# An S5 filter gated with linear attention on one core: the gate's logit as a column of K's weight, the skip term as products for all tiles, named buffers, and another list of the order

## The chip, the cores and the metric

The kernel runs on one core of a Trainium2 chip. The metric is the device time of one execution in microseconds. In the profile PE is the matrix engine (TensorE), PEld its loading of the stationary operand, DVE the vector engine, ACT the scalar engine, POOL the engine GpSimd and SP the engine that here only issues DMAs.

## The reference

```python
x = A_x                                            # [1, 2048, 512]
g = sigmoid((x * gate_w).sum(-1, keepdims=True))   # one number for each row
# a: S5 filter, 512 complex states
Lam_bar = exp(exp(log_dt) * Lam)                   # Lam = Lambda_re + 1j * Lambda_im
B_bar = ((Lam_bar - 1) / Lam)[:, None] * (B_re + 1j * B_im)
h[t] = Lam_bar * h[t - 1] + B_bar @ x[t]           # over the 2048 rows
a = 2 * real(h @ (C_re + 1j * C_im).T) + x * Dskip
# b: linear attention, 32 heads of 16
q, k, v = split(x @ wqkv)
pq, pk = q @ w_phi, k @ w_phi                      # per head, 16 x 16
phi = concat(softmax(p), softmax(-p))              # 32 features, for q and k
b = (phi_q @ (phi_k.T @ v)) / (phi_q @ sum(phi_k) + 1e-6) @ wo
out = g * a + (1 - g) * b
```

All inputs and the output are bf16.

## The kernel before, in words

The 2048 rows are taken as 16 tiles of 128. Row t belongs to residue t mod 8, and a tile holds the rows of one residue, half of them each. `xT` holds x transposed, with the 512 columns of x on the partitions in four pieces, and is the stationary operand of most products.

**The attention.** K and Q aren't built from `wqkv` and `w_phi` one after the other. The two weights are folded into one at the start (tokens `f0` to `f3` for K, `w0` to `w3` for Q, line 441ff.), and since a softmax doesn't change when one number is taken from all logits of a head, only 15 differences of each head are computed: 32 x 15 = 480 columns, in 8 blocks of 60. The product for a tile (`k0` to `k15`, `q0` to `q15`, line 493) is evacuated from PSUM into `Xq`, whose row has 8 blocks of 64: four zeros, then the 60 differences. K is handled in five groups of tiles (`KGROUPS`), Q in four (`G0` to `G3`). For a group, DVE takes the maximum and minimum over the features of a head as a tree (tokens `x` and `n`, line 544) and subtracts (lines 555, 561), ACT exponentiates (`e`, line 567), and DVE and POOL's adding DMAs sum (`s`). K's features times V with a column of ones, `vx`, are accumulated over all tiles into two banks of PSUM (`a0` to `a4`, line 627). Q's features are transposed by DMAs from the queue of SP into `phT` (line 613). Q's rows in `Xq` take the place of K's.

**The gate.** Beside the KV product, each tile has four products of one column (line 631): a piece of `xT` against a column `gw_b` of the gate's weight, into spare columns of the second PSUM bank. `st_G` (line 802) clamps the negated logit into `nge` and makes the gate `G` of it, for all tiles at once. The attention's reciprocal carries exp(-logit) as a bias (line 901), so that a product with the gate at the very end does for both halves.

**The filter.** Rows of eight residues turn the recurrence into one over 256 steps. `b` and `g` are its input products, `p`, `h`, `H`, `c`, `l` and `z` scale, rotate and scan the states; products with a diagonal are scaled copies on ACT or DVE (`scaled`, lines 444 and 446), and sums of large tiles are adding DMAs that POOL issues (line 529).

**The output.** For a tile, `y` accumulates eight products of 512 columns (states against C, line 875) in one bank, `o` computes the attention's numerators and denominators into two other banks (line 894), ACT takes the logarithm `ld` and the exponential `rd` (lines 898, 901), DVE multiplies into `on` (line 907), SP's queue transposes `on` of two tiles into `oT` (token `O`, line 930), and `t` adds four products with Wo to y's bank and evacuates it times `G` into `ot` (lines 943 to 951), which `R` stores. The skip term x * Dskip comes in two ways. For twelve tiles `y` adds four products of `xT` with a diagonal matrix `Dd` (line 882). For the four tiles of `XD`, 8 to 11, x is loaded once more, DVE computes `xd` = x * G * Dskip (line 913), and the evacuation adds it (line 947).

**What sets the order.** Each token of the list `ORDER` runs one more piece of a generator. `@` gives the PSUM banks, and `:D` puts the piece's evacuation or scaled copy on DVE, otherwise on ACT. The instructions go to their engines in the order of the list, and each engine keeps it:

```python
for tok in ORDER.split():
    tok, _, banks = tok.partition("@")
    tok, _, eng = tok.partition(":")
    sel["eng"] = "dve" if eng == "D" else "act"
    sel["banks"] = [int(b) for b in banks]
    next(st[tok])
```

At the start, `Z` are warm-up products on zeros, `W` and `T` transposes on PE of K's weight and of two tiles of x, `V` and `V2` transposes of small vectors (`vec_n`: the filter's three; `vec_m`: Dskip and the gate's weight). `Lx`, `Lb`, `Lc` and so on are loads; the transposing ones are issued by SP.

Of the kernel before, what the change touches and what calls it, by code (L numbers as in the profile page):

```python
# [24 lines left out]
B:D Lk Lk Z@0 Lx Z Z Z Z Z Z W00@1 Z B B B W01@2 W01 W01:D W00 W00 W10@0 Lx W11@3 Lx T0@4 B W11 T0 f1@2 Lx Lx f0@1 f0  # L25
W10:D f1:D T1@5 T1:D f2@3 f2 f3@0 f3:D k0@6 x0z:D Lx k1@7 V@3 V P U U k1 k1 k0 k0 P k3@3 P2 P P2 U P2 U k6@2 P2 P2 x0
Lx Lb Lx Lb P4 n0 P4 k3 x0 V2@6 P4 V2 P3 i3 gw P2 n0 P3 k5@7 x0 i3 x0 Lc k5 k9@3 k9 i0 Ld k2@0 M n0 i3 i3 k10@1 i3
k4@3 i0 M k2 i0 i0 i0 M Lb k10 i2 M k6 n0 k4 k7@0 k7 i2 Lb k8@7 i1 i2 x0 i1 i1 k13@6 M2 k11@0 n0 i2 k8 i1 x1 n1 x1 D
n1 x1 b200@1 i2 i1 L i0:D x1 D c1:D n1 Lc Lc i3:D n1 k11 e0 b010@7 b010 c0:D x1 n1 i2:D b200 x2 s0 c0:D s0 k12@3 k12
x2 g200@2 g200 n2 c1 b100@0 s0 b100 x2 b001@5 n2 Lv b000@7 Lc i1 b000 b111@4 b111 x2 n2 s0 n2 g000@2 b001 s0 c3:D  # L30
b011@3 b101@7 e1 x2 n2 g000 g000 Lx g001@5 g001 x3 s1 v1@4 b011 c3 s0 c2:D c2:D c1:D k14@2 g010@3 g010 Lo e2 x3 n3 s1
k13 D v0@0 v1 s1 g011@1 x3 c3:D g011 x3 g001 g011 v0 e2 k15@0 g011 g010 c0:D Lq Lq g010 s1 n3 k14 w2@6 c3 s0 D k15 n3
a0@54 s2 a0 g011 x3 n3 g011 Ld g010 g201@2 b101 Ld n3 s1 w2 g010 z0 b201@1 b201 z0 b110@7 n4 s1 x4 g101@3 g201 l2:D s2
s2 x4 n4 e3 z0 z0 w1@6 w1 b110 g100@2 g100 g101 g101 g100 s2 s2 s2 g111@1 l2:D l2:D g111 n4 g110@0 g110 e3 g110 g111
v2@2 v3@3 x4 n4 g110 g111 g111 g110 l2:D z0 v2 z0 v3 w3@2 s1 z0 g111 s3 g110 w0@7 w3 a1 a1 x4 c1 g301@6 z0 z1 z1 x4 w0
c2 g301 s3 g300@2 g300 z0 q3@7 q3 n4 e4 v5@6 z0 s2 s2 q2@2 s3 e4 q0@7 q0 z1 z1 l2:D z1 H0:D z1 s3 z1 z1 s4 v4@3 v4 q2
# [42 lines left out]
def kernel(  # L79
# [779 lines left out]
    def st_y(n):  # L859
# [23 lines left out]
        if n not in XD:  # L883
            yield
# [138 lines left out]
```

## Time and profile before

| | before |
|---|---|
| time of the runs, median (lowest to highest), 3 runs | 148.97 us (148.59 to 149.18) |
| the profiled execution: its span | 147.2 us |
| PE busy | 140.8 us, 96% |
| DVE busy | 135.1 us, 92% |
| ACT busy | 123.4 us, 84% |
| POOL busy | 45.4 us, 31% |
| packets of the transposing and plain DMAs of SP and ACT (queue q1) | 15.05 MB, 52.7% of 16 engines |
| granted clock of PE | 1.00 in all slices |

The span is the profiled execution's own time from its first to its last instruction; the profile gives no other time for that execution, and the runs' median stands 1.8 us above it. A row of the profile names a line of the kernel, an engine, an operation and tiles with their shapes. An engine is busy while an instruction runs; waits are idle times with the instruction that ended them. [...]

### The profile page before, as it was taken

How to read it: one execution, taken by the hardware profiler on the slowest of the kernel's cores; microseconds unless marked ns; L12 is line 12 of the kernel's file. 1: busy time of each engine (PE TensorE's matmuls, PEld its weight loads, DVE VectorE, ACT ScalarE, POOL GpSimd, SP SyncE). 2: the span in 40 equal slices, each digit the busy share in tenths (PEclk: the TensorE clock that was granted, in tenths of full speed). 3: DMA queues.
4: the chain of work that ended last, by engine and by line, in shares of the span. 5: the costliest groups of instructions: out<-in, count | busy, mean ns of one | idle time of the engine just before them, and what ended most of it. 6: DMA issues, size and time to landing. Idle time of an engine off the chain costs nothing.

```text
span 147.2 us, 2881 instructions
## 1 busy us (share of the span) xinstructions
PE 140.8 (96%) x1014; PEld 73.3 (50%) x1014; DVE 135.1 (92%) x330; ACT 123.4 (84%) x222; POOL 45.4 (31%) x61
## 2 busy tenths in 40 slices
PE   6999999999999999999999999999979999999990
PEld 2744444444544644554454656545445554545650
DVE  2879999999999999999999999999998999979740
ACT  3479999999999999999999999999988997912110
POOL 7503600003138195797545353051003003000000
PEclk9999999999999999999999999999999999999999
DMA  5999998990846586789878969969988999999643
GB/s 123 233 184 170 181 179 160 239 290 2 195 94 90 88 114 99 80 127 169 131 111 141 144 90 191 123 126 164 208 179 153 192 214 159 199 180 271 129 111 114
DMA packets 56047, 22.63 MB, mean 154 GB/s; under 512 B 44768, under 2 KB 54880, under 8 KB 56032
## 3 DMA queue, kind: packets, MB, share of 16 engines
q1 hardware_dynamic: 47584, 15.05, 52.7%
q0 software_dynamic: 7504, 7.09, 33.8%
q10 hardware_dynamic: 944, 0.31, 0.9%
q8 instruction: 8, 0.13, 0.4%
q14 instruction: 7, 0.06, 0.1%
HBM read 2.51 MB, written 2.10 MB: 31 GB/s over the span
## 4 chain that ended last, share of the span: by engine, by line
DVE 45%; PE 36%; ACT 9%; DMA 4%; issue 3%; DVEq 0%
PE PS L875 17%; PE PS L943 8%; DVE EE L597 6%; DVE mn L544 5%; DVE mx L544 5%; DMA phT<-EE 4%; DVE EE L555 4%; DVE sq L575 4%; DVE EE L561 3%; PE PS L894 3%; PE PS L493 3%; PE PS L324 2%; DVE w L723 2%; ACT vx L137 2%; ACT Xq L137 2%
## 5 line engine op out<-in xcount | busy, mean ns | idle before, releaser
L567 ACT ACTIVATE EE<-EE 128x2048 bf16<-128x2048 bf16 x16 | 30.3, 1933 | 0.4 <-DVE EE L561 0.4
L493 PE MATMUL PS<-WKV,xT 128*128 128x480 bf16 (+1 forms) x128 | 29.2, 372 | 0.2 <-ACT WKV L137 0.2
L493 PEld LDWEIGHTS <-xT 128*128 128x128 bf16 x192 | 18.1, 97 | 19.7 <-issue 0.9
L137 ACT CAST Xq<-PS 128x480 bf16<-128x480 f32 x32 | 17.5, 592 | 0.2
L653 PE MATMUL PS<-xT,BT 128*128 128x512 bf16 x64 | 16.2, 379 | 0.0
L875 PE MATMUL PS<-C,H 128*128 128x512 bf16 x64 | 15.6, 379 | 0.0
L943 PE MATMUL PS<-Wo,oT 128*128 128x512 bf16 (+2 forms) x68 | 15.5, 366 | 0.0
L493 PE MATMUL PS<-Wq,xT 128*128 128x480 bf16 x64 | 14.9, 365 | 0.0
L641 PE MATMUL PS<-xT,BT 128*128 128x512 bf16 x64 | 14.8, 379 | 0.0
L529 POOL DMA_DIRECT2D C<-CT x4 | 6.8, 1712 | 18.1 <-DVE CT L446 18.1
L907 DVE TENSOR_TENSOR on<-PS,rd 128x512 bf16<-128x512 f32 x16 | 10.9, 684 | 1.0 <-ACT rd L901 0.9
L529 POOL DMA_DIRECT2D eb<-dg x4 | 4.8, 1201 | 22.3 <-ACT dg L444 10.9
L949 ACT ACTIVATE ot<-PS,G 128x512 bf16<-128x512 f32 (+1 forms) x10 | 6.3, 647 | 4.7 <-PE PS L943 4.7
L641 PEld LDWEIGHTS <-BT 128*128 128x128 bf16 x64 | 6.3, 98 | 7.5
L561 DVE TENSOR_TENSOR EE<-mn,Xq 128x2048 bf16<-128x2048 bf16 (+1 forms) x9 | 9.9, 1095 | 0.0
L555 DVE TENSOR_TENSOR EE<-Xq,mx 128x2048 bf16<-128x2048 bf16 (+1 forms) x9 | 9.8, 1094 | 0.0
L575 DVE TENSOR_TENSOR sq<-EE 128x2048 bf16<-128x2048 bf16 (+1 forms) x9 | 9.8, 1094 | 0.0
L943 PEld LDWEIGHTS <-oT 128*128 128x128 bf16 x68 | 6.4, 98 | 6.7
L898 ACT ACTIVATE ld<-PS 128x32 f32<-128x32 f32 x16 | 3.0, 202 | 7.8 <-PE PS L894 7.8
L597 DVE TENSOR_TENSOR EE<-EE,rc 128x2048 bf16<-128x2048 bf16 x8 | 9.6, 1210 | 0.0
L653 PEld LDWEIGHTS <-BT 128*128 128x128 bf16 x64 | 6.1, 97 | 6.9 <-issue 0.2
L137 ACT CAST vx<-PS 128x512 bf16<-128x512 f32 x16 | 9.5, 618 | 0.0
(196 smaller groups left out, 329.7 us busy)
## 6 DMA issues: line engine op xcount, KB each, us to landing
out_dram<-ot SPq DMA_DIRECT2D x7, 256.0 KB, 2.5
C<-CT POOLq DMA_DIRECT2D x4, 256.0 KB, 5.2
eb<-CT POOLq DMA_DIRECT2D x4, 256.0 KB, 4.3
eb<-dg POOLq DMA_DIRECT2D x4, 256.0 KB, 4.3
sq<-sq POOLq DMA_DIRECT2D x3, 256.0 KB, 3.8
WKV<-in_B_wqkv_dram SPq DMA_DIRECT2D x1, 512.0 KB, 4.9
Wo<-in_B_wo_dram SPq DMA_DIRECT2D x1, 512.0 KB, 4.1
WKV<-in_A_x_dram SPq DMA_DIRECT2D x2, 256.0 KB, 4.8
```

What stands on the lines that cost most here:

```text
L137: nc.scalar.copy(out=out_ap, in_=in_ap)
L493: MM(out=pt[:], lhsT=xT[:, kt, ti * P:(ti + 1) * P], rhs=W[:, kt, :], start=(kt == 0), stop=(kt == KT - 1))
L544: VT(out=dst, in0=cur[:, :, :, 0:n, :], in1=cur[:, :, :, n:2 * n, :], op=op)
L555: VT(out=half(EE, 0), in0=X5, in1=live["mx", p].to_broadcast([P, L, 8, Dh, 4]), op=ALU.subtract)
L561: VT(out=half(live["EE", p], 1), in0=live["mn", p].to_broadcast([P, L, 8, Dh, 4]), in1=X5, op=ALU.subtract)
L567: aexp(out=EE[:, l_:l_ + 2], in_=EE[:, l_:l_ + 2], func=ACT.Exp)
L575: VT(out=sq.rearrange("p q x i -> p x q i"), in0=e4[:, :, 0:2], in1=e4[:, :, 2:4], op=ALU.add)
L597: VT(out=E5[:, u:u + 2], in0=E5[:, u:u + 2], in1=rc[:, u:u + 2].to_broadcast([P, 2, 2 * NB, Dh, 4]), op=ALU.mult)
L641: MM(out=pb[:], lhsT=BT[:, ri, kt, j * P:(j + 1) * P], rhs=cells(kt, 2 * pr), start=(kt == 0), stop=(kt == KT - 1))
L653: MM(out=pgq[:], lhsT=BT[:, ri, kt, js], rhs=cells(kt, r1), start=(kt == 0), stop=(dst == 0 and j in LJ and kt == KT - 1))
L875: MM(out=py[:], lhsT=hs[j][ri], rhs=C2[:, 1 - ri, j, c:c + w], start=(j == 0 and ri == 0), stop=False)
L943: MM(out=py[:], lhsT=oT[:, g, :], rhs=Wo[:, g, c:c + w], start=False, stop=(g == HG - 1))
```

## The change

1. **The gate's logit becomes a column of K.** K's folded weight grows from 480 to 488 columns: each of the 8 blocks has a 61st column. That of block 0 holds the gate's weight, copied from a transposed `vec_m`, which now has only the gate's four rows; the other seven are zeros. K's evacuation writes 61 columns of a block, and `Xq`'s blocks become 66 wide, 132 bytes instead of 128. `st_G` reads the logits from there instead of from PSUM. The 64 products of one column and the cast `gw_b` go.
2. **The skip term by products for all tiles.** `XD` goes, with the two reloads of x, four `xd` and four adding evacuations. Tiles 8 to 11 get the four products with `Dd` too, and are evacuated as the others. `Dd` is made from the broadcast row `Drow` by a token of its own, `Dk`.
3. **Buffers by name.** Tiles that the pools handed out in turn are now made once and handed out in turn by `rotating`.
4. **Another list `ORDER`.** All its rows are new.

```diff
-B:D Lk Lk Z@0 Lx Z Z Z Z Z Z W00@1 Z B B B W01@2 W01 W01:D W00 W00 W10@0 Lx W11@3 Lx T0@4 B W11 T0 f1@2 Lx Lx f0@1 f0
+B:D B B B B Z@0 Z Z Z Z Z Z Z V2@7 Lk Lk W01@2 W00@1 V2 W00 W01 W10@3 W11@4 W00 W01:D W11 W10:D Lx T0@7 V@2 V P f0@5
...
-XD = (8, 9, 10, 11)
+    def rotating(pool, bufs0):
+        slots = {}
+
+        def tile_of(shape, dtype, name, bufs=None):
+            s = slots.setdefault(name, [[], 0])
+            if not s[0]:
+                s[0] = [pool.tile(shape, dtype, name=f"{name}{k}", bufs=1) for k in range(bufs or bufs0)]
+            s[1] += 1
+            return s[0][(s[1] - 1) % len(s[0])]
+
+        return tile_of
...
-    vec_m = const.tile([8, P], BF16, name="vec_m")
+    vec_m = const.tile([4, P], BF16, name="vec_m")
-    Wk2, Wv = WKV[:, 0, :, 0:DF], WKV[:, 1]
+    KX = 8 * (4 * (Dh - 1) + 1)
+    Wk2, Wv = WKV[:, 0, :, 0:KX], WKV[:, 1]
+    Wk3 = Wk2.rearrange("p k (hh x) -> p k hh x", hh=8)
+    nc.vector.memset(Wk3[:, :, 1:8, DF // 8], 0.0)
+    nc.gpsimd.dma_start(out=vec_m[:], in_=gate_w.rearrange("(j p) -> j p", p=P))
-    Xq = pR.tile([P, NTI, D], BF16, name="Xq")
+    XW = 4 * Dh + 2
+    Xq = pR.tile([P, NTI, 8, XW], BF16, name="Xq")
...
-        for n in XD[::2]:
-            k, r = n - XD[0], order[n] // 2
-            w = min(2, len(XD) - k)
-            nc.sync.dma_start(out=WKV[:, k // 4, k % 4:k % 4 + w, :], in_=x_tiles[:, r, 0:w])
-            yield
...
-    for n, src in enumerate((A_Dskip, gate_w)):
-        nc.gpsimd.dma_start(out=vec_m[4 * n:4 * n + 4, :], in_=src.rearrange("(j p) -> j p", p=P))
...
-        nc.vector.tensor_copy(out=vec[:, 3:5, :].rearrange("p n j -> p (n j)"), in_=pvt[:])
-        nc.gpsimd.affine_select(out=Dd[:], in_=dsk.unsqueeze(2).to_broadcast([P, KT, P]), compare_op=ALU.is_equal,
+        nc.vector.tensor_copy(out=Wk3[:, :, 0, DF // 8], in_=pvt[:])
+        yield
+
+    def st_Dk():
+        nc.gpsimd.affine_select(out=Dd[:], in_=Drow[:].rearrange("p (k q) -> p k q", k=KT), compare_op=ALU.is_equal,
                                 fill=0.0, base=0, pattern=[[0, KT], [-1, P]], channel_multiplier=1)
...
-    def st_gw():
-        nc.vector.tensor_copy(out=gw_b[:], in_=vec[:, 4, :])
...
-        evac(xrel(ti), pk[:].rearrange("p (hh x) -> p hh x", hh=8))
+        evac(xrel(ti, 4 * Dh + 1), pk[:].rearrange("p (hh x) -> p hh x", hh=8))
...
-            for kt in range(KT):
-                MM(out=live["acc"][1][:, 4 * KVW + ti:4 * KVW + ti + 1], lhsT=xT[:, kt, ti * P:(ti + 1) * P],
-                   rhs=gw_b[:, kt:kt + 1], start=False, stop=(n_ == NTI - 1 and kt == KT - 1), skip_group_check=True)
...
-        VS(out=nge[:], in0=live["acc"][1][:, 4 * KVW:4 * KVW + NTI], scalar1=-Z_MAX, scalar2=-1.0, op0=ALU.max, op1=ALU.mult)
+        VS(out=nge[:], in0=Xq[:, :, 0, 4 * Dh], scalar1=-Z_MAX, scalar2=-1.0, op0=ALU.max, op1=ALU.mult)
...
-        for kt in range(KT if n not in XD else 0):
+        for kt in range(KT):
...
-    def st_u(n):
-        ti = order[n]
-        live["xd", n] = pools["op"][1].tile([P, D], F32, name="xd", bufs=2)
-        nc.vector.scalar_tensor_tensor(out=live["xd", n][:], in0=xl(n), scalar=G[:, ti:ti + 1], in1=Drow[:], op0=ALU.mult, op1=ALU.mult)
-        yield
...
-            if n in XD:
-                nc.vector.scalar_tensor_tensor(out=ot, in0=py[:], scalar=G[:, ti:ti + 1], in1=live["xd", n][:, c:c + w], op0=ALU.mult, op1=ALU.add)
-            elif sel["eng"] == "act":
+            if sel["eng"] == "act":
                 nc.scalar.mul(out=ot, in_=py[:], mul=G[:, ti:ti + 1])
```

What moves is shown at three places. On POOL at the start, where `ident` and `identf` are identity matrices, the rows before are these:

```order
masks.py:199 AFFINE_SELECT ident_74<-ident_74 128x128
L164 DMA vec_n_64<-in_A_Lambda_im_dram 4x128
L164 DMA vec_n_64<-in_A_Lambda_re_dram 4x128
L164 DMA vec_n_64<-in_A_log_dt_dram 4x128
masks.py:197 MEMSET identf_152 128x128
masks.py:199 AFFINE_SELECT identf_152<-identf_152 128x128
L278 IOTA iot_151 128x256
L279 MEMSET Xq_118 128x96x4
L281 DMA vec_m_65<-in_A_Dskip_dram 4x128
L281 DMA vec_m_65<-in_gate_w_dram 4x128
```

and now these:

```order
masks.py:199 AFFINE_SELECT ident_75<-ident_75 128x128
L176 DMA vec_m_65<-in_gate_w_dram 4x128
L178 DMA vec_n_64<-in_A_Lambda_im_dram 4x128
L178 DMA vec_n_64<-in_A_Lambda_re_dram 4x128
L178 DMA vec_n_64<-in_A_log_dt_dram 4x128
masks.py:197 MEMSET identf_153 128x128
masks.py:199 AFFINE_SELECT identf_153<-identf_153 128x128
```

The gate's vector is the first load of POOL instead of the last, and that of Dskip has gone.

On PE at the end of the warm-up, before (`C2` holds K's weight there, and PS is PSUM):

```order
L324 LDWEIGHTS warm_69
L324 MATMUL PS_61<-warm_69 128x512
L307 LDWEIGHTS C2_68
L307 MATMUL PS_61<-ident_74,C2_68 128x128
L307 LDWEIGHTS C2_68
```

and now:

```order
L327 LDWEIGHTS warm_69
L327 MATMUL PS_61<-warm_69 128x512
L339 LDWEIGHTS vec_m_65
L339 MATMUL PS_61<-ident_75,vec_m_65 128x4
L310 LDWEIGHTS C2_68
L310 MATMUL PS_61<-ident_75,C2_68 128x128
```

The transpose of the gate's vector stands between the warm-up products and the first transpose of K's weight; before, it stood between two K products further on.

On ACT ahead of the first reciprocal (`ld`, `rd`), the rows before:

```order
L567 ACTIVATE EE_1214<-EE_1214 128x2048 x2
L137 CAST Xq_118<-PS_61 128x8x60
L805 ACTIVATE G_90<-nge_91 128x16
L444 ACTIVATE CT_129<-H1_117,dgs_126 128x1024
L898 ACTIVATE ld_1373<-PS_61 128x32
L898 ACTIVATE ld_1385<-PS_61 128x32
L901 ACTIVATE rd_1391<-ld_1373,nge_91 128x32
L444 ACTIVATE dg_124<-H3_116,dgs_126 128x512 x2
L137 CAST Xq_118<-PS_61 128x8x60
L901 ACTIVATE rd_1412<-ld_1385,nge_91 128x32
```

and now:

```order
L569 ACTIVATE EE0_353<-EE0_353 128x2048 x2
L135 CAST Xq_119<-PS_61 128x8x60 x2
L446 ACTIVATE dg_125<-H3_117,dgs_127 128x512
L446 ACTIVATE CT_130<-H1_118,dgs_127 128x1024
L446 ACTIVATE m51_1177<-H3_117,dgs_127 128x1024
L446 ACTIVATE n50_1178<-H3_117,dgs_127 128x1024
L135 CAST Xq_119<-PS_61 128x8x60 x2
L446 ACTIVATE dg_125<-H3_117,dgs_127 128x512
L895 ACTIVATE ld0_1265<-PS_61 128x32
L895 ACTIVATE ld1_1266<-PS_61 128x32
L898 ACTIVATE rd0_1271<-ld0_1265,nge_92 128x32
L898 ACTIVATE rd1_1272<-ld1_1266,nge_92 128x32
```

More scaled copies stand ahead of the first pair, and the two `rd` of the first two tiles follow each other. Counted from the start of the list, ACT has ahead of its first `rd`: of scaled copies of 1024 elements, CT from CT 3 instead of 1 and CT from H 4 instead of 3; of those of 512 elements, 3 of dg instead of none and 3 of C instead of 2, but 1 of mc instead of 3, 1 of ms instead of 2 and 3 of phT instead of 4; 3 of ms of 256 elements instead of 1; 3 fold evacuations of K instead of 2; 28 evacuations of K and Q into `Xq` instead of 30, and 7 of H instead of 8; and not the exponential of `G`. PE has ahead of its first product with Wo 32 products of 512 columns for y instead of 40, and none of the 64 of one column.

166 lines of the change are left out of this document (79 added, 87 removed).

## The prediction

> **What bounds the kernel now.** I read the busy times first, then a table of stretches of the span, then the waits, then the chain that ended last and its place in time. In the table the columns are the stretch, its length, and the busy time of PE, PEld, DVE, ACT and POOL, then the granted clock, the DMA share and GB/s.
>
> ```profile
> PE 140.8 (96%) x1014; PEld 73.3 (50%) x1014; DVE 135.1 (92%) x330; ACT 123.4 (84%) x222; POOL 45.4 (31%) x61
> ...
> 0.00:9.00 9.00, 7.55 (x54) 4.35 (x55) 5.24 (x27) 3.77 (x6) 4.83 (x16) 1.00 0.85 179
> 9.00:20.00 11.00, 11.00 (x55) 5.19 (x54) 10.76 (x55) 10.53 (x25) 3.64 (x10) 1.00 1.11 168
> 20.00:40.00 20.00, 19.84 (x117) 9.60 (x116) 20.00 (x49) 19.99 (x33) 1.45 (x2) 1.00 0.84 178
> 40.00:60.00 20.00, 20.00 (x127) 10.11 (x126) 19.96 (x38) 19.64 (x33) 12.13 (x14) 1.00 0.64 100
> 60.00:80.00 20.00, 20.00 (x140) 10.15 (x139) 20.00 (x44) 19.65 (x38) 14.04 (x14) 1.00 0.88 129
> 92.00:104.00 12.00, 11.99 (x96) 6.42 (x95) 12.00 (x28) 11.73 (x23) 2.40 (x2) 1.00 1.02 143
> 104.00:120.00 16.00, 14.94 (x116) 7.90 (x115) 15.37 (x32) 15.02 (x23) 1.20 (x1) 1.00 1.07 187
> 135.00:147.20 12.20, 8.50 (x74) 5.06 (x72) 6.08 (x9) 2.09 (x6) 0.00 (x0) 1.00 0.50 131
> ```
>
> From 9 to 104 us PE and DVE are both full, and ACT nearly so: it is idle for 0.47, 0.01, 0.36, 0.35 and 0.27 us in the rows up to 104, about 1.4 us together. So three engines run at their limit at once, and a microsecond that is taken from one of them is only won if the other two don't hold it back.
>
> ```profile
> PE PS L324 <- DVE warm L156: 1.2, 1, 1.2
> PE PS L894 <- DMA phT<-EE: 1.1, 1, 1.1
> PE PS L493 <- ACT WKV L137: 0.2, 1, 0.2
> ...
> ACT ld L898 <- PE PS L894: 7.8, 7, 2.5
> ...
> 101.92 6.49 DMA phT<-EE
> ```
>
> The waits of PE (total, times, longest) are three. The 1.1 us at L894 is the only one in mid-kernel, and the last row, from the chain that ended last, is its cause: a transposing DMA of the second Q group that was in flight for 6.49 us. ACT's 7.8 us for L894 lie behind 100 us, since the rows to 104 hold only 1.4 us of idle time. PE is thus the engine whose work sets the end, and the sum goes by PE: change of its work, plus new waits, minus old waits.
>
> **The gate column and the skip term on PE.** A timeline of PE gives the price of a product from where the next group starts.
>
> ```profile
> 90.33 0.24 PE L631 MATMUL PS<-gw_b,xT 128*128 128x1 bf16 x4
> 90.43 0.41 PE L627 MATMUL PS<-vx,EE 128*128 128x68 bf16 x8
> ...
> 94.53 0.39 PE L882 MATMUL PS<-Dd,xT 128*128 128x128 bf16 x4
> 94.76 0.81 PE L894 MATMUL PS<-KVm,phT 128*128 128x68 bf16 x16
> ...
> 104.42 1.03 PE L943 MATMUL PS<-Wo,oT 128*128 128x512 bf16 x4
> 105.29 1.03 PE L875 MATMUL PS<-C,H 128*128 128x512 bf16 x4
> ...
> L631 PEld LDWEIGHTS <-xT 128*128 128x128 bf16 x64 | 2.9, 96 | 0.0
> ```
>
> Four gate products take 90.43 - 90.33 = 0.10 us, so the 64 removed give back 16 x 0.10 = 1.6 us. Four Dd products take 0.23 us, so the 16 added for tiles 8 to 11 cost 4 x 0.23 = 0.92 us. Four 512-column products take 0.87 us, 0.42 ns a column; K's 64 products grow from 480 to 488 columns, 64 x 8 x 0.42 ns = 0.22 us. PE's work falls by 1.6 - 0.92 - 0.22 = 0.45 us, a third of a per cent.
>
> [...]
>
> **DVE and ACT.** Rows of single forms: busy, mean ns of one, idle before.
>
> ```profile
> L947 DVE SCALAR_TENSOR_TENSOR ot<-PS,G,xd 128x512 bf16<-128x512 f32 x4 | 3.0, 748 | 0.2
> L913 DVE SCALAR_TENSOR_TENSOR xd<-WKV,G,Drow 128x512 f32<-128x512 bf16 x4 | 3.0, 742 | 0.0
> L398 DVE CAST gw_b<-vec 128x4 bf16<-128x4 f32 x1 | 0.6, 601 | 0.0
> ...
> 11.89 0.75 POOL L339 TENSOR_SCALAR_AFFINE_SELECT Dd<-vec 128x512 bf16<-128x512 f32 x1 [3.96 <-DVE ssm_par L384]
> ...
> 95.52 1.23 ACT L444 ACTIVATE CT<-H,dgs 128x1024 bf16<-128x1024 bf16 x1
> 96.56 0.36 ACT L898 ACTIVATE ld<-PS 128x32 f32<-128x32 f32 x2
> 96.87 0.32 ACT L901 ACTIVATE rd<-ld,nge 128x32 f32<-128x32 f32 x1
> 97.10 1.32 ACT L444 ACTIVATE dg<-H,dgs 128x512 bf16<-128x512 bf16 x2
> 98.32 0.54 ACT L137 CAST Xq<-PS 128x480 bf16<-128x480 f32 x1
> ```
>
> DVE loses 3.0 + 3.0 + 0.6 = 6.6 us, nearly all of it the skip term behind 110 us, where PE waits for nothing of DVE's; that is worth nothing on the path. The four evacuations come back as plain scaled copies, on ACT or DVE. The two reloads of x (SP, 256 KB each) go too; no row shows anyone waiting for them. Dd is now made on POOL from the broadcast row, late, among the adding DMAs; POOL is busy for 14 of 20 us there, and the first Dd product is in the first y tile, after 90 us. I cost it at nothing; without that cover its 0.75 us (the row of L339) would push the adding DMAs behind it, and y, by that much.
>
> What the new list moves matters more. Ahead of the first reciprocal `rd` (the 96.87 row), ACT now has three more scaled copies of 1024 elements, two of C's and one of H's, at 96.56 - 95.52 = 1.04 us each. The 512-element ones change by four more and four fewer. The rest (two 256-element copies and a fold evacuation more; two Q evacuations, an H evacuation and the gate's exponential fewer, each 0.3 to 0.6) comes to -0.1. So 3.0 us more work stands ahead of the first `rd`. What PE has ahead of the first Wo product falls: eight y products of 512 columns (8 x 0.217 = 1.73) moved behind it, and 1.6 of gate products gone, 3.3 us. So PE gets there at 104.42 - 3.3 = 101.1, if nothing holds it.
>
> What it needs there is the first transposed `oT`. Its DMA and the DVE product before it:
>
> ```profile
> 100.26 0.68 DVE L907 TENSOR_TENSOR on<-PS,rd 128x512 bf16<-128x512 f32 x1
> ...
> L930 SPq DMA_TRANSPOSE oT<-on x9: 1189/1290/1758, 100.2 to 139.2; - x9
> ...
> DMA to landing us min/median/max: 3.0/3.5/5.0
> ```
>
> ACT has 3.0 us more to do and had 1.4 us of idle time to do it in, so the first `rd` starts at 96.87 + 3.0 - 1.4 = 98.5. Both `rd` of the pair now stand together, 0.25 apart, and two `on` at 0.68 follow: the transpose is issued 1.4 later, at 99.9. The first landing took 4.0 before (issued 100.2, PE started at 104.4), so `oT` is there at 103.9. PE waits 103.9 - 101.1 = 2.8 us, at that place or in pieces before it, wherever a Q evacuation or an `on` holds a bank. Its bounds: with all luck (`rd` 1 us earlier, since the idle time before 9 us may give as much again, and a landing of 3.0) 0.8; with no room used, the head's microsecond (below) on ACT as well, and a landing of 5.0, `rd` at 100.9 and a wait of 6.2.
>
> The old stall of 1.1 us at L894 I take as gone: the second group's transpose is issued by the same kind of feature work, but PE comes to it later by the wait just paid.
>
> **The head.** The gate vector is now needed ahead of K's folding, and it enters PE's order before the W transposes.
>
> ```profile
> 1.54 0.73 POOL L164 DMA_DIRECT2D vec_n<-in_A_Lambda_im_dram  x1 [0.18 <-issue]
> ...
> 1.25 3.17 PE L324 MATMUL PS<-warm 128*128 128x512 bf16 x7 [1.25 <-DVE warm L156]
> 4.85 1.29 PE L307 MATMUL PS<-ident,C 128*128 128x128 bf16 x14
> 7.80 0.97 PE L493 MATMUL PS<-WKV,xT 128*128 128x480 bf16 x4 [0.20 <-ACT WKV L137]
> ...
> vec_n<-in_A_Lambda_im_dram POOLq DMA_DIRECT2D x1, 1.0 KB, 3.9
> ```
>
> POOL's first DMA is issued at 1.54 and takes 3.9 us: now that is the gate vector, so PE's transpose of it starts at about 5.45. The W transposes queue behind it and start 0.6 later than at 4.85. The three `vec_n` follow, each 0.5 to 0.7 later, and their transpose too now stands ahead of the four folds; the fold evacuations, three of them on ACT in a row at 0.6, come out at about 9.5, and the first K tile ends near 9.7 instead of 8.8. I take +1.0 (0.6 to 1.3). It is not added: PE would come to the first Wo at 102.1 instead of 101.1 and wait 1.8 there instead of 2.8. If the cover goes (`oT` early), the head is what is left.
>
> **The sum.** -0.45 (work) + 2.8 (waits up to the first Wo, the head in them) - 1.1 (old stall) = +1.25 us. The profiled span is 147.2; the runs shown are 148.59 to 149.18 with a median of 148.97, so 1.8 us lie around the span. New span 148.45, time 148.97 + 1.25 = 150.2. The tail is as before: the last row of the table has PE at 8.5 of 12.2 us, and the last y and Wo products still stand last. Its own range, by the bounds of the wait (1.0, where the head remains, to 6.2): 148.97 - 0.45 - 1.1 + 1.0 = 148.4, up to 153.6; with a fifth cut off at the far end, where two bad cases must meet, 148.4 to 152.4.
>
> Half a per cent, 0.75 us, is about what can be told from no change: below 148.22 is faster, above 149.72 slower.
>
> **The rivals.**
>
> 1. *Faster.* The first `rd` comes no later than before. The waits are the place: if ACT's 3.0 us go into its idle time before 9 us as well (3.77 of 9 busy in the first row of the table), `rd` starts at 96.9, `oT` lands at 102.2 or, at the median of 3.5, at 101.8, and PE waits 0.7. Then -0.45 + 0.7 - 1.1 = -0.85, 148.1; with the head hidden as well and PE as dense as between 40 and 80 us, -1.55, 147.4. It decides at a first `rd` of about 97.0. For it: ACT had only small idle times but no long one, and DVE's spared work helps every `on`. Against it: 3.0 us counted against 1.4 found.
> 2. *No change.* PE's saving and the stall's are eaten by the head's +1.0 and small waits: -0.45 - 1.1 + 1.5 = 0, 149.0. For it: all three engines are full up to 104 us, so waits shift rather than vanish.
> 3. *The half clock lasts longer.* Seven warm-up products take 3.17 us, 0.45 each, where the 512-column ones later take 0.217. An idle 0.8 us between warm-up and transposes could keep PE at half speed for the folds and the first K tiles, 3 to 4 us of work: +1.5 on top of the sum, 151.6. Against it: the granted clock is 1.00 in all rows, and the W transposes here already ran with small gaps.
> [...]
>
> **Chances.** Forecast 0.50 (0.42 slower, 0.08 within half a per cent), faster 0.28 (0.23 faster, 0.05 within), no change 0.08, half clock 0.09, wide rows 0.05. Slower: 0.42 + 0.09 + 0.05 = 0.56; same: 0.08 + 0.05 + 0.08 = 0.21; faster: 0.23. The range goes from 147.6, which leaves out the best third of the faster case, to 152.3, which leaves out the forecast's worst tenth and half of the last two cases.
>
> **What would show it.** Right: PE's waits of 2 to 3.5 us between 85 and 105, with ACT or the `oT` transpose as releasers; a first `rd` at 98 to 99; no wait for `phT` near 107; L493's K groups at about 205 ns a product; the W transposes starting at 5.3 to 5.6. Wrong: a first `rd` at or before 97, no idle PE before the first Wo, or Xq's first tree level above 0.70 us. If PE waits 1 us for `phT` again, the term of -1.1 is wrong; if the warm-up's 0.45 shows in products after 7 us, the third rival holds.

## The result

| | before | changed |
|---|---|---|
| time of the runs, median (lowest to highest) | 149.07 us (148.59 to 149.46) | 155.98 us (155.19 to 157.65) |
| span of the profiled execution | 147.2 us | 153.8 us |
| PE, DVE, ACT busy | 140.8, 135.1, 123.4 us | 142.2, 131.0, 128.6 us |

The change makes the kernel 1.0439 times as long (95% interval 1.0386 to 1.0492), 6.5 us, where 150.2 with a range to 152.3 was forecast. The ratios leave out executions over 1.5% above a kernel's fastest, as the changed kernel's of 157.65 us at a granted clock of 0.976 (0.989 to 1.00 in its others), which matters for one kernel below, a_both, whose median is 155.5 but whose ratio goes by its two other runs, 152.6 and 152.9 at 0.996 and 0.997, and whose profile, of 158.15 us at 0.975, isn't used.

The same table by stretches as before, for the changed kernel (columns as in the prediction); the last row is of the kernel before, whose table there leaves out 80 to 92 us:

```profile
20.00:40.00 20.00, 18.40 (x86) 8.04 (x86) 17.81 (x43) 18.16 (x29) 1.31 (x1) 1.00 0.73 155
40.00:60.00 20.00, 19.86 (x130) 10.20 (x131) 19.41 (x37) 19.76 (x33) 9.26 (x11) 1.00 0.41 63
...
80.00:92.00 12.00, 10.19 (x96) 5.69 (x97) 12.00 (x34) 11.21 (x23) 9.49 (x7) 1.00 0.81 130
92.00:104.00 12.00, 11.52 (x73) 5.69 (x74) 10.77 (x26) 11.38 (x18) 3.60 (x3) 0.86 1.05 160
...
80.00:92.00 12.00, 11.96 (x141) 7.01 (x140) 12.00 (x32) 12.00 (x22) 4.55 (x5) 1.00 0.93 144
```

The three engines that were full up to 104 us now all have holes at 20 to 40 us; at 80 to 92 us PE and ACT have them, and at 92 to 104 us all three. PE was idle for 0.16 us at 20 to 40 and for 0.04 at 80 to 92 before; now it is for 1.6 and 1.8, and at 92 to 104 its granted clock is 0.86. The waits of PE name the places (total, times, longest):

```profile
PE PS L628 <- ACT vx L135: 1.7, 1, 1.7
PE PS L651 <- DMA BT<-in_A_B_re_dram: 1.5, 2, 0.8
PE PS L327 <- DVE warm L168: 1.3, 1, 1.3
PE PS L932 <- DMA oT<-on: 1.1, 1, 1.1
PE PS L873 <- ACT Xq L135: 0.4, 1, 0.4
PE PS L339 <- DMA vec_m<-in_gate_w_dram: 0.4, 1, 0.4
```

Before, the second of three rows was the wait for `phT` at L894. It is gone. In its place stand five new ones of 0.4 us or more: for B's transposing loads, for an evacuation of V, for `oT`, for an evacuation of Q, and in the head for the gate vector. Timelines of the changed kernel show the two large ones, on SP's queue, on POOL and on PE:

```profile
7.17 0.58 SPq L267 DMA_DIRECT2D WKV<-in_B_wqkv_dram  x1
7.80 1.23 SPq L263 DMA_TRANSPOSE CT<-in_A_C_re_dram  x1
9.08 7.53 SPq L246 DMA_TRANSPOSE xT<-in_A_x_dram  x4
16.66 3.35 SPq L252 DMA_TRANSPOSE BT<-in_A_B_re_dram  x2
...
80.77 3.74 POOL L345 TENSOR_SCALAR_AFFINE_SELECT Dd<-Drow 128x512 bf16<-128x512 bf16 x1
84.47 0.88 POOL L531 DMA_DIRECT2D H<-CT  x1
...
88.49 1.15 ACT L446 ACTIVATE CT<-H,dgs 128x1024 bf16<-128x1024 bf16 x1 [0.79 <-DMA H<-CT]
...
90.98 1.39 PE L628 MATMUL PS<-vx,EE 128*128 128x68 bf16 x32 [1.65 <-ACT vx L135]
92.20 4.07 PE L495 MATMUL PS<-Wq,xT 128*128 128x480 bf16 x11
```

The new list puts Q's and V's weight and a part of C ahead of most of x on SP's queue, so B's first load is issued at 16.66 (before: 10.06) and PE stands still for it at 20 to 22 us. And the diagonal `Dd`, made on POOL late in the kernel, takes 3.74 us instead of 0.75; the adding DMA behind it is issued at 84.47, ACT waits 0.79 us for its landing, V's evacuations behind that on ACT come late, and PE waits 1.65. Then PE runs Q products at half speed: 0.40 us from start to start in this stretch, 0.20 elsewhere. This half speed alone can't be what makes the kernel slow: another of its runs had a mean granted clock of 1.00 and took 156.43 us, more than the 155.53 of the profiled one.

### The profile page after: what moved, and what is told of

It reads as the page before. It is cut to its first block, busy times and chain, and to the rows that moved or that the text cites. A ratio compares the mean times of both kernels' runs of the same rounds, so it can differ in the third digit from the quotient of the medians.

```text
span 153.8 us, 2761 instructions
## 1 busy us (share of the span) xinstructions
PE 142.2 (92%) x951; PEld 72.9 (47%) x966; DVE 131.0 (85%) x320; ACT 128.6 (84%) x228; POOL 47.3 (31%) x60
## 4 chain that ended last, share of the span: by engine, by line
PE 42%; ACT 22%; SPq 11%; DMA 10%; DVE 5%; issue 5%; POOL 3%; ACTq 0%
PE PS L873 13%; PE PS L495 8%; PE PS L932 8%; SPq L246 6%; ACT EE L569 5%; PE PS L639 4%; DMA oT<-on 3%; ACT CT L446 3%; PE PS L651 3%; DMA H<-CT 3%; DMA BT<-in_A_B_re_dram 2%; ACT H L135 2%; PE PS L891 2%; SPq L257 2%; DMA H<-ms 2%
## 5 line engine op out<-in xcount | busy, mean ns | idle before, releaser
L495 PE MATMUL PS<-WKV,xT 128*128 128x488 bf16 (+1 forms) x124 | 29.9, 374 | 0.7 <-DMA WKV<-in_B_wqkv_dram 0.2
L135 ACT CAST Xq<-PS 128x488 bf16<-128x488 f32 (+1 forms) x30 | 17.0, 603 | 2.4 <-PE PS L495 2.1
L651 PE MATMUL PS<-xT,BT 128*128 128x512 bf16 x64 | 16.1, 379 | 1.5 <-DMA BT<-in_A_B_re_dram 1.5
L639 PE MATMUL PS<-xT,BT 128*128 128x512 bf16 x64 | 16.5, 379 | 0.0
L495 PE MATMUL PS<-Wq,xT 128*128 128x480 bf16 x64 | 16.4, 397 | 0.0
L873 PE MATMUL PS<-C,H 128*128 128x512 bf16 x61 | 15.1, 379 | 0.5 <-ACT Xq L135 0.4
L938 ACT ACTIVATE ot<-PS,G 128x512 bf16<-128x512 f32 (+1 forms) x13 | 8.6, 674 | 5.5 <-PE PS L932 5.4
L531 POOL DMA_DIRECT2D C<-CT x4 | 5.3, 1326 | 21.2 <-DVE T2c L448 20.8
L446 ACT ACTIVATE CT<-H,dgs 128x1024 bf16<-128x1024 bf16 x9 | 10.6, 1178 | 0.8 <-DMA H<-CT 0.8
```

The source lines that it names most:

```text
L135: nc.scalar.copy(out=out_ap, in_=in_ap)
L446: nc.scalar.mul(out=out_ap, in_=in_ap, mul=s_)
L495: MM(out=pt[:], lhsT=xT[:, kt, ti * P:(ti + 1) * P], rhs=W[:, kt, :], start=(kt == 0), stop=(kt == KT - 1))
L531: nc.gpsimd.dma_start(out=out_ap, in_=in_ap, accum_op=ALU.add)
L639: MM(out=pb[:], lhsT=BT[:, ri, kt, j * P:(j + 1) * P], rhs=cells(kt, 2 * pr), start=(kt == 0), stop=(kt == KT - 1))
L651: MM(out=pgq[:], lhsT=BT[:, ri, kt, js], rhs=cells(kt, r1), start=(kt == 0), stop=(dst == 0 and j in LJ and kt == KT - 1))
```

## The experiments

Times are ratios to the kernel before with the 95% interval, from runs on the same chip, and medians. The changed kernel is 1.0439, 155.98 us.

### The late deliveries, one at a time

**a_dd**: the diagonal early.

```diff
 s2 Lx
+Ld
 k15@0 k15 ... x0z:D
+Dk
 s1 ... v8@3
-Ld
 c2 c2 ... q11
-Dk
```

> The changed kernel with the broadcast row of Dskip loaded before Wo and the diagonal made on POOL at about 42 us instead of 81 us, ahead of other adding DMAs; nothing else differs. Theory 1 (two late deliveries hold PE: the B transposes at 20 us and the adding DMA behind the 3.74 us of POOL at 81 us): PE's wait of 1.8 us for vx before 91 us goes, and the half-clock stretch at 93 us with it, so 152.0 to 153.7 against 155.5. Theory 2 (the new list is unbalanced between PE, ACT and DVE as such, and any wait removed comes back later): within 0.7 of the changed kernel. Theory 3 (a part of the change other than the list costs the time): no difference either.

Measured: 1.0387 (1.0348 to 1.0427), 154.96 us. The instruction took 0.98 us at 40.86 instead of 3.74, and PE's wait for `vx` fell from 1.7 to 0.8. By the ratios the time fell by 0.8 us, and the two intervals overlap, so that even this isn't clear. The waits of this kernel show why it wasn't more: one for the second group's transpose stands there anew.

```profile
PE PS L651 <- DMA BT<-in_A_B_re_dram: 1.6, 2, 1.0
...
PE PS L891 <- DMA phq<-EE: 1.2, 1, 1.2
...
PE PS L628 <- ACT vx L135: 0.8, 1, 0.8
```

**a_ld**: B's loads two places earlier.

```diff
-n1 Lc w0@1 w2@4 v3 M n1 M x0 c1:D v0@2
+n1 w0@1 w2@4 v3 M n1 M x0 v0@2
...
-i0 Lx k7 D x1 D x1 k4 k9 Lb Lb Lb i0
+i0 k7 D x1 D x1 k4 k9 Lb Lb Lx Lb i0
...
-Lb b000@2
+Lb Lc b000@2
...
+c1:D
 c0:D
```

> The changed kernel with the transposing loads of B two places earlier on SP's queue (the first half of C's real part and x's tiles 10 and 11 go behind them); the scaled copy of C that reads the moved load follows it. Theory 1: PE's 1.9 us of waits for BT at 20 to 22 us fall to below 0.5, and the time to 153.5 to 154.3. Theory 2: the waits move to another place, within 0.7 of the changed kernel (155.5).

Measured: 1.0395 (1.0348 to 1.0442), 155.17 us. The wait didn't go, it changed its name: the first input product reads x's tiles 10 and 11 too, which the edit had put behind B.

```profile
PE PS L651 <- DMA xT<-in_A_x_dram: 1.9, 1, 1.9
PE PS L628 <- ACT vx L135: 1.8, 1, 1.8
```

So this run says nothing on what early loads are worth; a_fix, below, tries it again. It shows one thing by the way. PE waited 1.76 us for `vx`, as long as in the changed kernel, but its 16 Q products behind that took 3.40 us, 0.21 each: the half speed followed such a wait in some executions and not in others.

**a_both**: both edits.

```diff
 s2 Lx
+Ld
 k15@0 k15 ... x0z:D
+Dk
...
+i0 k7 D x1 D x1 k4 k9 Lb Lb Lx Lb i0
```

> Both edits together. Theory 1: the gains add, 150.0 to 152.0. Theory 2: above 154. The rest, up to the kernel before, would be the head and the waits at the first numerators.

Measured: 1.0258 (1.0223 to 1.0292), from two runs. That is 2.7 us less than the changed kernel, with intervals that don't meet, and more than the two edits gave singly. It isn't explained here.

**a_fix**: the diagonal early, and SP's queue for x and B as in the kernel before.

```diff
-Lq k0@3 ... Lq i3 Lv v3@7 ... Lc w0@1 w2@4 v3 ... c1:D v0@2 ... w2 ... v0 ... v2@0 v2 ... w0
+k0@3 ... i3 ...
...
-Lb b000@2
+Lb Lq Lq Lv Lc b000@2
...
+w0@1 w2@0 w0 w2 v3@1 v0@0 v3 v0 v2@1 v2
 k8@0
+c1:D
 c0:D
```

> The changed kernel with the diagonal made at 42 us as in the first study, and with Q's weight, V's weight and the first half of C loaded behind B on SP's queue; the two folds of Q and the three V products that need them go behind the first input products on PE. So x's tiles and B stand on SP's queue as early as in the kernel before. Theory 1: PE's 2 us before its first input products go and the vx wait is below 1: 151.5 to 153.0 against 155.5. Theory 2 (the waits move elsewhere): 154 or more.

Measured: 1.0493 (1.0427 to 1.0558), no better than the changed kernel. B's first load is now issued at 10.25 and lands at about 14.4, and no wait for it is left. In its place:

```profile
PE PS L639 <- ACT Xq L135: 1.8, 1, 1.8
PE PS L495 <- ACT Wq L135: 1.7, 1, 1.7
...
PE PS L339 <- DMA vec_m<-in_gate_w_dram: 1.2, 1, 1.2
```

With B in time PE comes to ACT's evacuations of K sooner, and stands there for as long. The second row comes from this edit itself: the moved folds and V products go through two banks in turn. The third is a landing that varies from run to run (last section). So here waits that were taken away came back as others behind them. That doesn't settle theory 1, that the two late deliveries are the loss: this edit brought a wait of its own, its first K product came 1.3 us later than the changed kernel's (9.85), and a_both did win 2.7 us. How much of the loss the two deliveries are stays open.

### ACT's work ahead of the first reciprocal

**a_act**: the three scaled copies off ACT.

```diff
-p00 p11 S0 S0 y3@2 y3 y3 h2 h2 q15@6
+p00 p11:D S0 S0 y3@2 y3 y3 h2:D h2:D q15@6
```

> The changed kernel with three scaled copies of 1024 elements moved from ACT to DVE, all three shortly ahead of the first reciprocal (ACT -3.1 us, DVE +1.4). Theory P (the prediction's: ACT's added work ahead of the first rd delays it, and PE's products with Wo behind it): first rd 1.5 to 3 us earlier than 102.4, time 152.5 to 154.0 against 155.5. Theory 2' (ACT is late there because PE and the loads were late before, and DVE waits as well): first rd and time within 0.7.

Measured: 1.0481 (1.0449 to 1.0514), 156.25 us, no gain. The first `rd` starts at 102.71, against 102.42 in the changed kernel, although ACT has 3.1 us less to do ahead of it. ACT's busy time at 92 to 104 us falls from 11.38 to 8.46, and its wait for PE ahead of the first `ld` grows from 0.37 to 3.10 (the changed kernel's row last):

```profile
92.00:104.00 12.00, 11.52 (x78) 5.70 (x76) 11.70 (x28) 8.46 (x15) 3.60 (x3) 0.86 1.10 163
102.36 0.45 ACT L895 ACTIVATE ld<-PS 128x32 f32<-128x32 f32 x2 [3.10 <-PE PS L891]
...
102.07 0.45 ACT L895 ACTIVATE ld<-PS 128x32 f32<-128x32 f32 x2 [0.37 <-PE PS L891]
```

So the prediction's main term, ACT's added work, isn't what makes the first `rd` late. ACT is early and waits for PE, which is late by its own earlier waits. ACT's work is the next limit, though: in a_dd, where PE's wait for `vx` is shorter, the first `rd` comes at 100.92 and ACT doesn't wait for PE ahead of it.

**a_all**: these copies on DVE, the diagonal early, the identity ahead of POOL's loads (as in g_idf, below).

```diff
+p00 p11:D S0 S0 y3@2 y3 y3 h2:D h2:D q15@6
...
 s2 Lx
+Ld
 k15@0 k15 ... x0z:D
+Dk
...
     make_identity(nc, ident[:])
+    identf = const.tile([P, P], F32, name="identf")
+    make_identity(nc, identf[:])
```

> The same three copies on DVE, the diagonal made at 42 us, and the f32 identity ahead of POOL's loads. If the causes found so far add up: 155.5 - 1.5 to 2.5 (ACT) - 0.7 (diagonal) - 0.5 (head) = 151.8 to 152.8. If the waits at B's loads take up the head's gain: 152.5 to 153.5.

Measured: 1.0455 (1.0405 to 1.0504), 155.77 us. The first `rd` comes at 99.96, 2.5 us earlier, and PE's last group of products starts only 0.76 us earlier. What the earlier identity gives can't be read from this execution, whose first K product came at 10.01 instead of 8.59, behind folds at half speed (the rivals, below). The gain of `rd` is lost on the way:

```profile
PE PS L932 <- DMA oT<-on: 1.6, 2, 1.0
...
PE PS L891 <- DVE on L904: 1.2, 1, 1.2
```

### The parts without the list

**b_parts**: every part of the change with the list of the kernel before. The tokens of the parts that went are left out; what stands in their place:

```diff
-T1:D f2@3 ... V2@6 P4 V2 ... gw ... e0 ... y8 ... t8
+T1:D V2@7 V2 f2@3 ... P4 ... e0 Dk ... y8 y8 ... t8:D
```

> All parts of the change except the list: gate column, products with the diagonal for all tiles, named buffers, and the gate vector loaded first, with the kernel before's list (its tokens for the parts that went are left out; the transpose of the gate vector stands ahead of the folds f2 and f3, the diagonal is made on POOL before the adding DMAs, the four evacuations of tiles 8 to 11 stay on DVE). If the list alone costs the time (theories 1 and 2): 148.0 to 149.2, PE's work 0.45 us less than before. Theory 3: above 150.5.

Measured: 1.0228 (1.0199 to 1.0256), 152.23 us. This splits the loss: the parts cost 3.2 us on a list on which they should have won 0.5, and the new list costs 3.3 more. Three runs take the parts singly, on the list of the kernel before.

**p_buf**: the named buffers alone.

```diff
+    def rotating(pool, bufs0):
...
-    ft = ft_g.__enter__()
+    ft_tile = rotating(ft_g.__enter__(), 1)
...
-        mc = sw.tile([P, 2, NC], BF16, name="mc")
+        mc = sw([P, 2, NC], BF16, name="mc")
```

> The kernel before with the buffers named outright as the one edit. Same instructions in the same order. Theories A and B: within 0.3 of the kernel before. Theory C' (other buffers in turn give other waits): 150 or more.

Measured: 0.9972 (0.9946 to 0.9999), 148.91 us. They cost nothing.

**p_skip**: products with the diagonal for all tiles alone (the list without the tokens that went, the four evacuations on DVE).

```diff
-XD = (8, 9, 10, 11)
+XD = ()
```

> The kernel before with the products with the diagonal for all 16 tiles as the one edit (no reloads of x, no xd; the four evacuations stay on DVE as plain scaled ones; the diagonal is made as in the kernel before). PE gets 16 products of 128 columns more, 0.9 us, DVE loses 3 us, SP two loads. Theory A (PE's work sets the end): +0.9, 149.9. Theory B (the stretch from 100 to 120 us is paced by the transposes, so the products fall into waits): 148.7 to 149.3. Theory C (this part is where the 3.2 us of all parts together come from): 151 or more.

Measured: 1.0049 (1.0026 to 1.0073), 150.26 us: 0.7 us, near the 0.9 of theory A. The 16 products count nearly in full, and the 3 us that DVE is spared are worth little.

**p_gate**: the gate column (with named buffers and the diagonal from the row of Dskip), tiles 8 to 11 with `xd` as before. As b_parts, but:

```diff
+XD = (8, 9, 10, 11)
...
-y8 y8 ... t8:D
+u8 y8 ... t8
```

> The gate column, the named buffers and the diagonal from the broadcast row, on the kernel before's list; the skip term of tiles 8 to 11 as before (x loaded again, xd on DVE). PE loses 1.6 and gets 0.22, DVE loses 0.6. Theory A: -1.4 + 0.5 for the head, 148.1. Theory B (the products of one column were in waits or beside them and their removal is given back as waits for transposes): 149.0 to 149.6. Theory C'' (the gate column costs by the wider rows of Xq or by the head): 150.5 or more.

Measured: 1.0090 (1.0062 to 1.0117), 150.66 us: 1.4 us slower, where the removed products should have made it 0.9 faster. The stretch from 20 to 104 us, of the kernel before:

```profile
20.00:104.00 84.00, 83.79 (x614) 43.28 (x613) 83.97 (x187) 83.01 (x144) 34.58 (x33) 1.00 0.84 138
```

and with the gate column:

```profile
20.00:104.00 84.00, 81.87 (x540) 41.76 (x547) 83.61 (x187) 82.65 (x143) 35.33 (x34) 1.00 0.82 135
```

PE's busy time falls by 1.9 us (some ten products lack a record, 0.05 us each by the author's estimate), DVE's stays at 83.6 of 84. PE does less in the same time and waits. Its longest waits there are two for V's evacuations by ACT, 0.5 and 0.4 us. The first product with Wo starts at 105.40 instead of 104.42, and 0.59 us of that is the head (first K product at 8.39 instead of 7.80). p_gate and p_skip lose 1.4 and 0.7 us, 2.1 together, where all parts at once lost 3.2; the rest isn't explained. Theory D is that DVE, full in this stretch, holds PE back. Two runs test it.

**b_dve** and **g_dve**: eight DVE instructions, 3.1 us, left out at 25 to 41 us, of the kernel before and of p_gate. The maximum takes the minimum's place, so the output isn't the reference's.

```diff
+        if p in (2, 3):
+            for _ in range(4):
+                yield
+            live["mn", p] = live["mx", p]
+        else:
-        yield from tree(X5, L, ALU.min, "mn", ("mn", p))
+            yield from tree(X5, L, ALU.min, "mn", ("mn", p))
```

> The kernel before without the four steps of the minimum's tree in the third and fourth group of K (eight DVE instructions of 0.68, 0.41, 0.28 and 0.21 us, 3.1 us; the maximum takes the minimum's place, so the output isn't the reference's). Theory D (from 20 to 104 us DVE sets the pace together with PE and ACT): PE and ACT are as full as DVE in this kernel, so little is gained: 0 to -1. If DVE alone set the pace: -2.5 to -3. If only the transposes behind 100 us set it: 0.

> The same eight DVE instructions left out of the kernel with the gate column (the third kernel of the study before, 150.7). Theory D: there PE has 1.4 us less to do and its saving was held back by DVE, so now it shows: 1.0 to 2.0 below that kernel, and clearly more than the same edit brings to the kernel before. If the transposes behind 100 us alone set the pace: 0 as in the other one.

Measured: b_dve 0.9978 (0.9954 to 1.0002), g_dve 1.0025 (1.0009 to 1.0041), against 1.0000 and 1.0090. The same 3.1 us of DVE are worth 0.3 us in the kernel before and 1.0 us where the gate's products are gone. The intervals of p_gate and g_dve don't touch, but the two gains differ by 0.6 us with an uncertainty as large. The profiles, one of each kernel, speak against theory D. Rows of p_gate, then of g_dve:

```profile
105.40 1.03 PE L949 MATMUL PS<-Wo,oT 128*128 128x512 bf16 x4
112.59 1.47 SPq L938 DMA_TRANSPOSE oT<-on  x1
PE PS L949 <- DMA oT<-on: 1.6, 1, 1.6
...
105.12 1.03 PE L954 MATMUL PS<-Wo,oT 128*128 128x512 bf16 x4
112.32 1.47 SPq L943 DMA_TRANSPOSE oT<-on  x1
PE PS L954 <- DMA oT<-on: 0.7, 1, 0.7
```

The stretch that DVE was to hold back is only 0.3 us shorter. The other 0.9 us come behind it: the transpose that is issued at 112.59 lands after 6.3 us, the one at 112.32 after 5.4, and PE waits for both. So what keeps PE from its saving isn't shown to be DVE.

**g_idf**: p_gate with the f32 identity made ahead of POOL's loads.

```diff
     make_identity(nc, ident[:])
+    identf = const.tile([P, P], F32, name="identf")
+    make_identity(nc, identf[:])
...
-    identf = stg.tile([P, P], F32, name="identf", bufs=1)
-    make_identity(nc, identf[:])
```

> The kernel with the gate column, with the f32 identity made on POOL ahead of POOL's first four loads instead of behind them. Theory H (the head's 0.5 us come from the fourth load's issue on POOL, ahead of the identity, for which DVE's masks and through them the folds wait): DVE's first wait of 2.0 us falls to below 1, the first K product starts at 7.8 or earlier instead of 8.4, and as DVE is dense from there the whole 0.5 to 0.8 us come off: 149.9 to 150.2. If the head is held by the transposes of the weight or by the vector loads: no change.

Measured: 1.0062 (1.0032 to 1.0091), 150.06 us. In the profile of p_gate the identity starts on POOL at 3.82, behind the fourth load, and DVE waits 2.0 us for it:

```profile
3.31 0.52 POOL L179 DMA_DIRECT2D vec_n<-in_A_log_dt_dram  x1
3.82 0.22 POOL masks.py:197 MEMSET identf<- 128x128 f32 x1
```

In g_idf DVE's reduction of it starts at 2.08 and the first K product at 7.63 instead of 8.39. So the identity behind POOL's loads holds up the head of p_gate, and the fourth load's issue, 0.52 us, delays an identity that has nothing to do with the gate; the edit takes it ahead of all four loads, so that it doesn't price the fourth alone. The gain in time, 0.6 us, has the size expected, but its interval overlaps that of p_gate.

**b_idf** and **pb_idf**: the same edit as in g_idf, on the kernel before and on p_buf.

> The kernel before with the f32 identity made on POOL ahead of POOL's loads, the one edit. Theory H: DVE's first wait of 1.6 us falls to about 1, its masks come 0.5 to 1 us earlier; the folds also wait for the transposed weight, which lands when it lands, so 0.2 to 0.6 us: 148.5 to 148.9 beside 149.1. If POOL's later vector loads matter instead: 149.1 to 149.5.

> The same with the buffers named outright, which alone gave 0.9972 of the kernel before: 148.2 to 148.6 if both add, the best version if so; 148.9 to 149.3 if the 0.3% were the spread of the runs.

Measured: b_idf 1.0007 (0.9985 to 1.0028), 149.30; pb_idf 0.9988 (0.9964 to 1.0012), 148.70. Neither can be told from the kernel before. No version here beats it clearly.

### What the diagonal waits for on POOL

**x_probe**: the changed kernel with four pairs of instructions that make a diagonal nobody reads.

```diff
+    def st_Dp():
+        while True:
+            nc.gpsimd.affine_select(out=Dx[:], in_=warm[:].rearrange("p (k q) -> p k q", k=KT), compare_op=ALU.is_equal,
+                                    fill=0.0, base=0, pattern=[[0, KT], [-1, P]], channel_multiplier=1)
+            nc.gpsimd.affine_select(out=Dx[:], in_=ldt.unsqueeze(2).to_broadcast([P, KT, P]), compare_op=ALU.is_equal,
+                                    fill=0.0, base=0, pattern=[[0, KT], [-1, P]], channel_multiplier=1)
+            yield
```

> The changed kernel with four pairs of extra instructions on POOL that make a diagonal into a tile nobody reads, one from bf16 zeros as the changed kernel does it and one from a broadcast f32 column as the kernel before did it: at about 20 to 36 us, after the first adding DMA, right behind the diagonal at 81 us, and at the end. If the form sets the time, all bf16 ones take 2 to 3.7 us and all f32 ones 0.75. If what DVE does beside them sets it, both forms vary with the place. Theory 1 of the first study (POOL's 3.74 us reach PE through the adding DMA): the pair at 81 us adds its whole length to PE's wait for vx, 1.8 + 1.5 to 7 us.

Measured, one run: 156.85 us. The rows of POOL at 81 us, the diagonal itself and the pair behind it:

```profile
81.48 3.74 POOL L346 TENSOR_SCALAR_AFFINE_SELECT Dd<-Drow 128x512 bf16<-128x512 bf16 x1
85.19 0.81 POOL L362 TENSOR_SCALAR_AFFINE_SELECT Dx<-warm 128x512 bf16<-128x512 bf16 x1
86.07 0.90 POOL L364 TENSOR_SCALAR_AFFINE_SELECT Dx<-vec 128x512 bf16<-128x512 f32 x1
...
82.36 0.41 DVE L719 TENSOR_TENSOR ms<-vv,T2s 128x512 bf16<-128x512 bf16 x1
84.11 0.68 DVE L730 TENSOR_TENSOR_SCAN w<-ssm_par,mc 128x256 bf16<-128x256 f32 x1
84.71 0.79 DVE L457 TENSOR_SCALAR CT<-H,dgs 128x1024 bf16<-128x1024 bf16 x1
```

The same form takes 3.74 and then 0.81 us, and 1.02, 1.11 and 1.38 at the other places, so the form doesn't set the time. From 80.8 to 84.1 DVE ran `TENSOR_TENSOR` instructions with two inputs from SBUF without a gap (one of them shown); the diagonal ended only at 85.2, after DVE had come to a scan at 84.11. And the scaled copy of DVE that ran then took 0.79 instead of the 0.49 of another of its size. The extra 1.7 us on POOL raised PE's wait for `vx` from 1.7 to 2.8, so a delay on POOL does reach PE there, by 1.1 us of the 1.7.

## Why the prediction was wrong

The direction was right and the size was not: +1.25 us forecast, +6.5 measured, outside the range. By the spans, 153.8 us instead of 148.45, 5.3 us are missing. The forecast had PE at its first product with Wo at 103.9, the wait there included, and it came at 108.15: 4.2 us of the 5.3 were lost ahead of that place, and the wait of 1.1 us for `oT` stands behind it.

**The work of PE, -0.45.** The count holds, its worth does not. The prediction put the whole saving on the path, since PE's work "sets the end". Its own first table had three engines full up to 104 us. 1.6 us fewer products gave no gain in p_gate, and relieving DVE moved its first product with Wo by only 0.3 us; which engine holds PE there stays open.

**ACT's work ahead of the first `rd`, 2.8 us of wait at the first Wo.** This step failed. The first `rd` came at 102.42 instead of 98.5, the first `oT` landed at 107.9, and PE came to it at 108.15 without a wait: it had waited before, 1.5 us for B's loads, 1.65 for `vx` and 0.4 for a Q evacuation, and run 16 Q products in 4.93 us where a_ld needed 3.40. Taking the three copies away moved nothing (a_act). One sign of being right came true by luck: PE did wait for ACT for 2.1 us between 85 and 105 us, but most of that was for V's evacuations behind a late adding DMA.

**The old stall, -1.1.** The wait for `phT` at L894 did go. A wait of 1.1 to 1.6 us for an `oT` stands in its place, in the changed kernel as in p_gate. The step "PE comes to it later" was right, and it was not asked which transpose is late next.

**The head, +1.0.** The gate vector's transpose started at 5.27 (5.45 forecast) and the first K product at 8.59 instead of 7.80, so 0.8. The size was right, but in this execution half speed in the weight's transposes has a part in it (below). That POOL's extra load also delays an identity and through it DVE's masks was missed.

**The diagonal, nothing.** This failed, and it was the one cost for which the prediction named its cover. POOL had been called busy for 14 of 20 us there, and 0.75 us taken from a row at 11.89 us. It took 3.74.

**SP's queue.** The prediction has no term for it, though the list moves four loads ahead of x and B. This is the step left out: 1.5 us of PE's waits, and three engines with holes at 20 to 40 us. That these waits are worth their length in time isn't shown (a_ld, a_fix).

**The rivals.** The third rival, half speed in the head, came true in some executions. Of the transposes and the folds, the rows of the changed kernel, then the transposes of a_ld and the folds of a_act, whose edits leave the head alone:

```profile
5.38 1.87 PE L310 MATMUL PS<-ident,C 128*128 128x128 bf16 x16
7.51 1.01 PE L453 MATMUL PS<-BD,Xq 128*128 128x120 bf16 x16
...
5.16 1.10 PE L310 MATMUL PS<-ident,C 128*128 128x128 bf16 x16
...
8.14 1.78 PE L453 MATMUL PS<-BD,Xq 128*128 128x120 bf16 x16
```

The changed kernel's transposes ran at half speed and its folds did not; in a_act both did, and the first K product came at 10.14 instead of 8.59. Little of that was left later: a_act waited less for B's loads, and its first product with Wo started at 108.44 instead of 108.15. The profile's granted clock reads 1.00 in these stretches, so the half speed shows only in the lengths. The chance of 0.05 for the wide rows of Xq, and their share in the upper end of the range, rest on no trace or run. The runs show that these rows, 132 bytes apart instead of 128, cost nothing worth naming: the first tree level of the maximum takes 677 ns after 678, that of the minimum 686 after 677, the subtraction 1220 after 1212, some 0.2 us over all (rows of the changed kernel, then of the kernel before).

```profile
L546 DVE TENSOR_TENSOR mx<-Xq 128x1024 bf16<-128x1024 bf16 x7 | 4.7, 677 | 0.0
L557 DVE TENSOR_TENSOR EE<-Xq,mx 128x2048 bf16<-128x2048 bf16 x7 | 8.5, 1220 | 0.0
...
L544 DVE TENSOR_TENSOR mx<-Xq 128x1024 bf16<-128x1024 bf16 x7 | 4.7, 678 | 0.0
L555 DVE TENSOR_TENSOR EE<-Xq,mx 128x2048 bf16<-128x2048 bf16 x7 | 8.5, 1212 | 0.0
```

**What stays open.** The list's own 3.3 us are seen in the profile as waits at 20 to 40 and 80 to 96 us, but a_both apart no edit of it has an interval that parts from the changed kernel's. Which of its moves is the cause can't be said; the runs only show that single waits in it are not additive. Nor is it known what holds PE in p_gate, and why all parts together cost 1.1 us more than p_gate and p_skip.

## What to carry to other kernels

Where a table of stretches shows three engines full at once, work taken from one of them may be worth nothing: here 1.4 us less on PE came out as idle time of PE. A delay at the start is worth what the later waits leave of it: on the old list a head 0.76 us shorter (g_idf after p_gate) brought the first product with Wo 0.75 us forward, on the new list a head 1.55 us longer (a_act) put it off by only 0.29. A step that is moved has to be priced on its new engine's queue at its new time, beside what the other engines do then: an instruction of the same kind took 0.75 us early and 3.74 us late. And before a wait is booked as gone, find the transfer that is late next.

## What the runs showed of the hardware

- In x_probe the diagonal on POOL, whose input is in SBUF, took 3.74 us from 81.48, while DVE ran instructions with two SBUF inputs one after the other until 84.1; the same form right behind it, at 85.19, took 0.81 us beside a scaled copy and a scan. In the changed kernel it took 3.74 us too, at 80.77, beside such instructions. It went the other way as well: in a_dd the diagonal took 0.98 us, and a step of DVE's tree that takes 0.22 in the changed kernel took 1.05 beside it. That the two engines hold each other up there is the author's reading of these rows.

```profile
40.86 0.98 POOL L345 TENSOR_SCALAR_AFFINE_SELECT Dd<-Drow 128x512 bf16<-128x512 bf16 x1
40.87 1.05 DVE L546 TENSOR_TENSOR mx<-mx 128x128 bf16<-128x128 bf16 x1
```

- The second transposing DMA behind a plain load on SP's queue held the queue until about the time that this load landed, in the three kernels named here. (Some transposes took longer without a plain load right ahead of them on the queue, as B's at 12.76 in the kernel before, 1.72 us; why isn't known.) In the changed kernel V's weight was issued at 7.17 and landed at 12.5; the transpose behind the next one was issued at 9.08 and held the queue for 3.3 us, to 12.4, instead of 1.3. In a_fix, with that load at 18.63, which landed 4.8 us later, it is the transpose at 21.34 that takes 2.02 us, to 23.4, and the five from 8.89 on take 1.3 to 1.4 each. In the kernel before it reads the same behind V's weight, which landed 4.9 us after its issue, at 27.8:

```profile
22.90 0.58 SPq L253 DMA_DIRECT2D WKV<-in_B_wqkv_dram  x1
23.53 1.23 SPq L249 DMA_TRANSPOSE CT<-in_A_C_im_dram  x1
24.80 2.81 SPq L232 DMA_TRANSPOSE xT<-in_A_x_dram  x1
```

- In the changed kernel PE ran at half speed for about 3.3 us behind an idle time of 1.65 us (0.40 us for a product of 480 columns, and a granted clock of 0.53 from 92.2 to 95.5), in a_act behind 1.74 us, and in a_ld, behind 1.76 us, it did not (0.21). So the length of the wait alone didn't decide it.
- The gate vector, 1 KB, landed between 5.0 us (a_ld) and 6.0 us (a_fix) after an issue at 1.55 in both. Here that is 1 us of spread ahead of the first K product.
